# A long convolution ahead of two expert layers: merged loads, decodings in three parts, an earlier filter transform, and the first tile's last rows kept on chip

## The chip, the cores and the metric

One core of a Trainium2 chip runs the kernel. The metric is the time of one execution in microseconds (us) on the device. Engines are called as in the profile: PE (matmul), PEld (its weight loads), DVE (vector), ACT (scalar), POOL (GpSimd), SP (the queue that issues most DMAs). Each engine works through its own instruction list in order.

## What is computed

```python
h_filt = (np.maximum(pos_emb @ w1, 0) @ w2) * exp(-0.01 * pos)   # 12480 x 128
u = x * v
y = irfft(rfft(u, 2 * S) * rfft(h_filt, 2 * S))[:S]              # causal convolution
x = x * y
h = x @ w_in;  g = P(h) / (Q(h) + 1e-06);  x = g @ w_out         # 128 -> 2048 -> 128
h = x @ w_in2; g = where(h >= 1, h, where(h <= -1, 0, (h + 1) ** 2 / 4))
out = g @ w_out2
```

P is a cubic and Q a quadratic in h with the weights `a` and `b`. The four weight matrices of the two layers arrive as float64, two 32-bit words a number.

## The kernel before

The convolution is an FFT in factors 256 and 49, as matmuls. It is written as `conv_transform`, whose order is that of the code (no scheduler moves it), and the two layers are the main loop that follows.

**Load stage** (L126 to L234). 49 rows are taken in 14 chunks of 1, 2, 4 (eleven times) and 2 (`CHS`). For a chunk, `loads` (L141) issues three DMAs on SP: `pt` (positions), `xt` and `vt`. `products` (L151) multiplies x and v on POOL, `mlp` (L159) makes the filter's hidden layer on PE and DVE, `parts` (L170) splits the result `st` into a high part (ACT) and a low part (DVE), the first transform runs on PE, ACT and DVE copy it to `so`, and ACT issues the write of `so` to `sd` in DRAM. The buffers of x and v hold three chunks.

**Filter stage** (L237 to L376). `sd` is read back in 34 groups of frequencies (`groups`): one of 1, 31 of 4, two of 2. `load(g)` reads `ru` from `sd`, `load_g(g)` the tables `gg`; both are issued by SP. For a group: `R` (L251) transforms the filter's rows on PE and splits the result (ACT makes the high part, DVE the low one, L88), `AB` (L260) applies w2, `U` (L274) transforms the signal on PE into the PSUM tile `up` (one buffer), `M` (L285) multiplies both on DVE (L298 to L302) and combines on POOL (L300 to L305), `Tr` transposes, `Inv` (L323) transforms back, and `co` is written to `cd` in DRAM. The steps are a software pipeline: step s works on group s + 1 in AB, s in U and M, s + 2 in R, s - 2 in Tr, s - 3 in Inv.

**Decodings.** `decode_steps` (L44) turns one block of the float64 weights `b` into float32 with six operations on DVE (`t`, `a`, `t`, `t`, then `k` and the last product) and an addition on POOL in their middle; for w_in blocks ACT then makes a high part and POOL the low one (L410 to L416). There are 32 such blocks. `fill(i)` (L106) first does the part behind the addition of block i - 1, then the part ahead of it of block i. Two run ahead of the steps, two in each of steps -2 and -1, and one in each step from 0 on, so that they end in step 25.

**Hand-over and main loop.** The column sums of the last weight matrix (`colsum`, L430) are made in the three tail steps. Then `X0` (L482) reads a tile of x (`xTt`) and of `cd` (`ct`) from DRAM, `XF` makes the last transform on PE, `XM` (L501) multiplies by x on DVE, `XH` and `XL` split it. The main loop takes 196 items of 1024 columns in the order of `ORDER`; in each, `h1` is the first layer's product on PE and `n1` (L551) the first of five operations on DVE. The second layer follows 11 items later.

Of the kernel before, what the change touches and what calls it, by code (L numbers as in the profile page):

```python
# [16 lines left out]
D = 128  # L17
# [13 lines left out]
CSP = [(0,), (1,), (2, 3)]  # L31
# [12 lines left out]
def decode_steps(nc, pool, src, n, dst):  # L44
# [32 lines left out]
def conv_transform(tc, ident, io, cd, fillers, colsum):  # L77
# [3 lines left out]
    xp, vp, posT, w1, w2, win, sgn, f1c, ggc = io  # L81
    with ExitStack() as ctx:
# [43 lines left out]
        with tc.tile_pool(name="ca", bufs=2) as ca, tc.tile_pool(name="cap", bufs=1, space=PSUM) as cap:  # L126
            xr = xp.rearrange("(b p m) d -> p b m d", b=NB, p=N1)
            vr = vp.rearrange("(b p m) d -> p b m d", b=NB, p=N1)
# [12 lines left out]
            def loads(c):  # L141
                m0, n = first[c], CHS[c]
                b = buf[c] = {}
                b["p"] = ca.tile([128, mx, N1], F32, name="pt", tag="pt", bufs=4)
                b["x"] = ca.tile([N1, NB, mx, D], F32, name="xt", tag="xt", bufs=XB)
                b["v"] = ca.tile([N1, NB, mx, D], F32, name="vt", tag="vt", bufs=XB)
                nc.sync.dma_start(b["p"][:, 0:n], posT[:, m0:m0 + n, :])
                nc.sync.dma_start(b["x"][:, :, 0:n], xr[:, :, m0:m0 + n, :])
                nc.sync.dma_start(b["v"][:, :, 0:n], vr[:, :, m0:m0 + n, :])

            def products(c):  # L151
# [3 lines left out]
                for k in range(NB):  # L155
                    nc.gpsimd.tensor_tensor(st[:, 0:n, k * 256:k * 256 + D], b["x"][:, k, 0:n], b["v"][:, k, 0:n],
                                            op=ALU.mult)

            def mlp(c):  # L159
# [3 lines left out]
                for j in range(n):  # L163
                    nc.tensor.matmul(rv[:, j], b["p"][:, j], w1b, start=True, stop=True)
# [25 lines left out]
            loads(3)  # L190
# [131 lines left out]
        def Inv(g, h):  # L322
# [4 lines left out]
            if h == 0:  # L327
                e["co"] = grp.tile([SL, 4, 256], F32, name="co", tag="co")
# [19 lines left out]

        for s in range(-2, ng + 3):
# [8 lines left out]
            on(R, s + 2)  # L358
# [18 lines left out]
def kernel(ctx, tc, xp, vp, xT, posT, w1, w2, win, sgn, f1c, ggc, fic,  # L377
# [390 lines left out]
```

## Time and profile before

| what | us |
|---|---|
| median of 3 runs (1693.29 to 1694.32) | 1693.93 |
| the profiled execution | 1693.96 |
| its span, first to last instruction | 1692.2 |
| PE busy in the span | 1581.5 (93%) |
| DVE busy | 1506.0 (89%) |
| ACT busy | 1426.9 (84%) |
| POOL busy | 1439.9 (85%) |

The page's first table gives busy time per engine over the whole span, which mixes three short stages and a long loop. To see what a stage is limited by one reads the windows (busy time of each engine in a stretch, with PE's granted clock and the share of the DMA engines), then the timeline of one engine: start, duration, instruction, and in brackets how long the engine was idle just before and what ended it.

### The profile page before, as it was taken

How to read it: one execution, taken by the hardware profiler on the slowest of the kernel's cores; microseconds unless marked ns; L12 is line 12 of the kernel's file. 1: busy time of each engine (PE TensorE's matmuls, PEld its weight loads, DVE VectorE, ACT ScalarE, POOL GpSimd, SP SyncE). 2: the span in 40 equal slices, each digit the busy share in tenths (PEclk: the TensorE clock that was granted, in tenths of full speed). 3: DMA queues.
4: the chain of work that ended last, by engine and by line, in shares of the span. 5: the costliest groups of instructions: out<-in, count | busy, mean ns of one | idle time of the engine just before them, and what ended most of it. 6: DMA issues, size and time to landing. Idle time of an engine off the chain costs nothing.

```text
span 1692.2 us, 18487 instructions
## 1 busy us (share of the span) xinstructions
PE 1581.5 (93%) x6310; PEld 1063.8 (63%) x6310; DVE 1506.0 (89%) x1524; ACT 1426.9 (84%) x1665; POOL 1439.9 (85%) x883
## 2 busy tenths in 40 slices
PE   6758888986799999999999999999999999999999
PEld 5747777873456656666666666566666666666566
DVE  5549999828999999999999999999999999999990
ACT  4433454546799999999999999999999999999996
POOL 4315676636599999999999999999999999999996
PEclk9877999999899999999999999999999999999999
DMA  9975777631000000000000000000000000000000
GB/s 337 380 259 174 217 216 218 173 100 38 19 13 25 25 1 25 26 26 25 13 13 25 25 26 26 1 25 26 25 25 26 0 26 25 26 16 7 0 7 16
DMA packets 59996, 113.20 MB, mean 67 GB/s; under 512 B 4599, under 2 KB 36607, under 8 KB 58493
## 3 DMA queue, kind: packets, MB, share of 16 engines
q1 hardware_dynamic: 45064, 80.35, 15.4%
q10 hardware_dynamic: 14724, 31.53, 5.1%
q8 instruction: 50, 0.82, 0.2%
q14 instruction: 46, 0.37, 0.1%
q0 software_dynamic: 112, 0.13, 0.0%
HBM read 73.46 MB, written 38.54 MB: 66 GB/s over the span
## 4 chain that ended last, share of the span: by engine, by line
PE 73%; DVE 13%; ACT 6%; DMA 5%; issue 2%; POOL 1%; SPq 0%; ACTq 0%; DVEq 0%; POOLq 0%
PE acc L479 36%; PE h L473 10%; PE h L475 10%; PE h L474 9%; PE acc L496 3%; DMA sd<-so 2%; PE up L281 2%; DVE m L299 1%; DVE m L302 1%; DMA vt<-in_vp_dram 1%; PE cp L334 1%; ACT z L537 1%; DVE t L67 1%; ACT f L533 1%; DVE n L555 1%
## 5 line engine op out<-in xcount | busy, mean ns | idle before, releaser
L546 POOL TENSOR_TENSOR w<-w,z 128x1024 f32<-128x1024 f32 x196 | 470.5, 2400 | 12.3
L632 POOL TENSOR_TENSOR y<-y,c 128x1024 f32<-128x1024 f32 x196 | 468.9, 2393 | 9.8 <-ACT c L628 4.7
L479 PE MATMUL acc<-g,wo 128*128 128x512 f32 (+1 forms) x800 | 373.2, 590 | 12.5 <-DVE g L576 12.5
L479 PE MATMUL acc<-y,wo 128*128 128x512 f32 (+1 forms) x800 | 368.0, 584 | 1.0 <-DVE o L642 0.9
L542 POOL TENSOR_SCALAR w<-z,ab 128x1024 f32<-128x1024 f32 x196 | 235.1, 1199 | 39.9 <-ACT z L537 38.8
L479 PEld LDWEIGHTS acc<-y,wo 128*128 128x128 f32 x800 | 151.6, 190 | 181.4 <-issue 173.0
L576 DVE SCALAR_TENSOR_TENSOR g<-r,n 128x1024 f32<-128x1024 f32 x196 | 240.1, 1225 | 20.7 <-PE h L475 0.5
L555 DVE SCALAR_TENSOR_TENSOR n<-n,co,h 128x1024 f32<-128x1024 f32 x196 | 250.9, 1280 | 6.1
L567 DVE SCALAR_TENSOR_TENSOR n<-n,co,r 128x1024 f32<-128x1024 f32 x196 | 250.2, 1277 | 1.8 <-ACT r L563 1.3
L551 DVE SCALAR_TENSOR_TENSOR n<-f,co,h 128x1024 f32<-128x1024 f32 x196 | 249.5, 1273 | 0.2 <-ACT f L533 0.2
L571 DVE SCALAR_TENSOR_TENSOR r<-w,r 128x1024 f32<-128x1024 f32 x196 | 239.6, 1222 | 0.0
L563 ACT ACTIVATE r<-L 128x1024 f32<-128x1024 f32 x196 | 213.3, 1088 | 20.5 <-DVE g L576 20.5
L479 PEld LDWEIGHTS acc<-g,wo 128*128 128x128 f32 x800 | 149.8, 190 | 123.3 <-issue 93.9
L473 PE MATMUL h<-x1hi,hi 128*128 128x512 f32 (+1 forms) x400 | 214.0, 535 | 13.7 <-DVE n L555 6.8
L559 ACT ACTIVATE L<-w 128x1024 f32<-128x1024 f32 x196 | 216.8, 1106 | 0.0
L615 ACT ACTIVATE y<-h 128x1024 f32<-128x1024 f32 x196 | 210.7, 1075 | 4.6 <-PE h L475 4.5
L537 ACT ACTIVATE z<-h 128x1024 f32<-128x1024 f32 x196 | 208.1, 1062 | 6.0 <-PE h L475 4.6
L533 ACT ACTIVATE f<-h 128x1024 f32<-128x1024 f32 x196 | 208.3, 1063 | 0.0
L473 PE MATMUL h<-x2hi,hi 128*128 128x512 f32 (+1 forms) x400 | 159.3, 398 | 5.9 <-DVE n L555 5.8
L626 ACT ACTIVATE c<-c 128x1024 f32<-128x1024 f32 x147 | 164.7, 1120 | 0.0
L621 ACT ACTIVATE c<-y 128x1024 f32<-128x1024 f32 x147 | 163.8, 1114 | 0.6
L475 PE MATMUL h<-x1lo,hi 128*128 128x512 f32 (+1 forms) x400 | 155.6, 389 | 0.6 <-POOL x1lo L512 0.6
(93 smaller groups left out, 2615.6 us busy)
## 6 DMA issues: line engine op xcount, KB each, us to landing
ru<-sd SPq DMA_DIRECT2D x31, 588.0 KB
sd<-so ACTq DMA_DIRECT2D x11, 1536.0 KB
ct<-cd SPq DMA_DIRECT2D x24, 512.0 KB
cd<-co ACTq DMA_DIRECT2D x30, 392.0 KB
gg<-in_ggc_dram SPq DMA_DIRECT2D x31, 300.1 KB
xTt<-in_xT_dram SPq DMA_DIRECT2D x24, 256.0 KB
out_dram<-o SPq DMA_DIRECT2D x24, 256.0 KB
xt<-in_xp_dram SPq DMA_DIRECT2D x11, 512.0 KB
```

The costliest lines, as they stand in the source:

```text
L473: nc.tensor.matmul(o, hi[:, f], x[0], start=True, stop=False)
L475: nc.tensor.matmul(o, hi[:, f], x[1], start=False, stop=True)
L479: nc.tensor.matmul(ps, W[l][2][:, f], g[:, k * w:(k + 1) * w], start=f == 0, stop=f == NF - 1)
L533: nc.scalar.activation(s1[i]["f"], s1[i]["h"], AF.Copy, scale=ra3)
L542: nc.gpsimd.tensor_scalar(s["w"], s["z"], ab[:, 1:2], ab[:, 0:1], op0=ALU.mult, op1=ALU.add)
L546: nc.gpsimd.tensor_tensor(s["w"], s["w"], s["z"], op=ALU.mult)
L551: nc.vector.scalar_tensor_tensor(s["n"], s["f"], a[2], s["h"], op0=ALU.add, op1=ALU.mult)
L555: nc.vector.scalar_tensor_tensor(s["n"], s["n"], a[1], s["h"], op0=ALU.add, op1=ALU.mult)
L567: nc.vector.scalar_tensor_tensor(s["n"], s["n"], a[0], s["r"], op0=ALU.add, op1=ALU.mult)
L571: nc.vector.scalar_tensor_tensor(s["r"], s["w"], 1.000001, s["r"], op0=ALU.add, op1=ALU.mult)
L576: nc.vector.scalar_tensor_tensor(s["g"], s["r"], 2.0, s["n"], op0=ALU.subtract, op1=ALU.mult, reverse0=True)
L632: nc.gpsimd.tensor_tensor(s["y"], s["y"], s["c"], op=ALU.add)
```

## The change

Loads: x, v and the positions are interleaved in DRAM, and one DMA reads a chunk of all three. Decodings: each is in three parts (ahead of POOL's addition, behind it, and the split), each done in a later `fill`; seven buffers for `b`; three run ahead of the steps, 23 in steps 2 to 33, four behind the tail steps and two behind the first tile's product. Filter transform: `R(s + 2)` stands behind `AB` and ahead of `Tr`, `U` and `M`. First tile: the rows that the last three groups make for it are copied from `co` to `ct0` in SBUF; the others are read from `cd` earlier; `begin` takes the place of the first `XF`, `XM`, `XH`, `XL`. `colsum` goes to item 8 of the main loop.

```diff
-CSP = [(0,), (1,), (2, 3)]
+PRE = 3
+POST = 4, 2
...
-        e["b"] = pool.tile([128, n, 2], I32, name="b64", tag="b64", bufs=3)
+        e["b"] = pool.tile([128, n, 2], I32, name="b64", tag="b64", bufs=7)
...
-        def fill(i):
-            nonlocal late
-            for fn in late:
-                fn()
-            late = []
-            fill_load(i + 2)
-            if i < len(fills):
+        def fill(n=1):
+            nonlocal done
+            for i in range(done, done + n):
+                fill_load(i + 1)
+                later()
                 for fn in fills[i][1:6]:
                     fn()
-                late = fills[i][6:]
+                waiting.append([fills[i][6:8], fills[i][8:]])
+                fill_load(i + 4)
+            done += n
+
+        def later():
+            for parts in waiting:
+                for fn in parts.pop(0):
+                    fn()
+            waiting[:] = [parts for parts in waiting if parts and parts[0]]
...
-                nc.sync.dma_start(b["p"][:, 0:n], posT[:, m0:m0 + n, :])
-                nc.sync.dma_start(b["x"][:, :, 0:n], xr[:, :, m0:m0 + n, :])
-                nc.sync.dma_start(b["v"][:, :, 0:n], vr[:, :, m0:m0 + n, :])
+                b["a"] = ca.tile([128, mx, 5, 128], F32, name="xt", tag="xt", bufs=XB)
+                nc.sync.dma_start(b["a"][:, 0:n], xvp[:, m0:m0 + n])
...
-                if c + 4 < nch:
-                    loads(c + 4)
+                if 3 < c + 3 < nch:
+                    loads(c + 3)
...
-                if c == nch - 4:
-                    for g in range(5):
-                        load_g(g)
-                    fill_load(0)
-                    fill_load(1)
+                if c == nch - 3:
+                    load_g(0)
+                    load_g(1)
+                    fill_load(PRE + 2)
...
-                e["co"] = grp.tile([SL, 4, 256], F32, name="co", tag="co")
+                e["co"] = grp.tile([SL, 4, 256], F32, name="co", tag="co", bufs=3)
...
             if h + 2 == n:
+                if g >= ng - TQ:
+                    for i in range(n):
+                        nc.sync.dma_start(ct0[k0 + i:k0 + i + 1], e["co"][0:TILES[0], i])
                 (nc.scalar if g < ng - TQ else nc.sync).dma_start(cdr[:, k0:k0 + n], e["co"][:, 0:n])
+                if g == ng - TQ:
+                    nc.sync.dma_start(ct0[0:k0], cd[0:k0, 0:TILES[0] // NB])
...
         for g in range(5):
             load(g)
-        for i in range(2):
-            fill(i)
-        done = 2
+            if g > 1:
+                load_g(g)
+        fill(PRE)
...
+        mid = len(fills) - PRE - sum(POST)
         for s in range(-2, ng + 3):
             if 5 <= s + 5 < ng:
                 load(s + 5)
                 load_g(s + 5)
             on(AB, s + 1)
+            on(R, s + 2)
             if s < ng:
                 on(Tr, s - 2, 0)
             on(U, s)
             on(M, s)
-            on(R, s + 2)
...
-                if s == ng:
-                    cs = ps.tile([128, 2, 512], F32, name="cs", tag="ap")[:, 0, 0:1]
-                for part in CSP[s - ng]:
-                    colsum(cs, part, 4)
-            for i in range(2 if s < 0 else 1):
-                fill(done)
-                done += 1
+            elif 0 < s and s * mid // (ng - 1) > (s - 1) * mid // (ng - 1):
+                fill()
+            if s == ng - 1:
+                fill_load(len(fills))
+        fill(POST[0])
+        begin(ps.tile([128, 2, 512], F32, name="x0", tag="ap")[:, 0, 0:TILES[0] * 128], ct0, xt0)
+        fill(POST[1])
+        while waiting:
+            later()
...
+    def begin(p, ct0, xt0):
+        for j in range(TILES[0]):
+            for r in range(2):
+                nc.tensor.matmul(p[:, j * 128:(j + 1) * 128], ct0[:, j // NB, r, j % NB * D:(j % NB + 1) * D],
+                                 fit[:, r], start=r == 0, stop=r == 1)
+        nc.vector.tensor_tensor(xt0, p, xt0, op=ALU.mult)
+        nc.scalar.copy(x10[0], xt0)
+        nc.gpsimd.tensor_tensor(x10[1], xt0, x10[0].bitcast(F32), op=ALU.subtract)
...
-        X0(0)
+        x1[0] = x10
         X0(1)
-        XF(0)
-        XM(0)
-        XH(0)
-        XL(0)
         for i in range(n + 24):
+            if i == 8:
+                colsum()
```

The order of instructions at three places. On SP, between the last chunks' loads and the `ru` loads; `b` are blocks of weights. Before:

```order
L147 DMA pt<-in_posT_dram 128x256
L148 DMA xt<-in_xp_dram 128x2x256
L149 DMA vt<-in_vp_dram 128x2x256
L121 DMA gg<-in_ggc_dram 98x196
L121 DMA gg<-in_ggc_dram 98x784 x4
L56 DMA b_782<-in_w_in_dram 128x512
L56 DMA b_784<-in_w_out_dram 128x2x256
L248 DMA ru<-sd 98x384
L248 DMA ru<-sd 98x4x384 x4
```

and with the change:

```order
L158 DMA xt<-in_xvp_dram 128x2560 x11
L158 DMA xt<-in_xvp_dram 128x1280
L136 DMA gg<-in_ggc_dram 98x196
L136 DMA gg<-in_ggc_dram 98x784
L57 DMA b_777<-in_w_in_dram 128x512
L57 DMA b_779<-in_w_out_dram 128x2x256
L57 DMA b_781<-in_w_in_dram 128x512
L57 DMA b_783<-in_w_out_dram 128x2x256
L57 DMA b_785<-in_w_in_dram 128x512
L256 DMA ru<-sd 98x384
L256 DMA ru<-sd 98x4x384 x2
L136 DMA gg<-in_ggc_dram 98x784
```

Three issues a chunk became one, three `gg` loads moved behind the `ru` loads, and three `b` loads moved ahead of them.

On DVE, one step of the filter stage (M is the four operations on `up`, `rs` the split of R). Before:

```order
L298 TENSOR_TENSOR m_2827<-up,ab 128x392
L299 TENSOR_TENSOR m_2825<-up,ab 128x784
L301 TENSOR_TENSOR m_2828<-up,ab 128x392
L302 TENSOR_TENSOR m_2826<-up,ab 128x784
L88 TENSOR_TENSOR rs_2844<-rp_2838,rs_2843 128x392
L72 TENSOR_SCALAR k<-b_2626 128x256
L73 SCALAR_TENSOR_TENSOR w_2865<-k,t 128x256
L67 TENSOR_SCALAR t<-b_2708 128x256
L68 TENSOR_SCALAR a<-b_2708 128x256
L69 SCALAR_TENSOR_TENSOR t<-b_2708,t 128x256
L70 SCALAR_TENSOR_TENSOR t<-b_2708,t 128x256
```

and with the change:

```order
L89 TENSOR_TENSOR rs_2617<-rp_2611,rs_2616 128x392
L306 TENSOR_TENSOR m_2638<-up,ab 128x392
L307 TENSOR_TENSOR m_2636<-up,ab 128x784
L309 TENSOR_TENSOR m_2639<-up,ab 128x392
L310 TENSOR_TENSOR m_2637<-up,ab 128x784
L73 TENSOR_SCALAR k<-b_2288 128x256
L74 SCALAR_TENSOR_TENSOR wo_78<-k,t 128x256
L68 TENSOR_SCALAR t<-b_2368 128x256
L69 TENSOR_SCALAR a<-b_2368 128x256
L70 SCALAR_TENSOR_TENSOR t<-b_2368,t 128x256
L71 SCALAR_TENSOR_TENSOR t<-b_2368,t 128x256
```

The split stands ahead of M, so the decoding follows M directly; in ten of the steps from 1 to 33 the decoding is missing.

On DVE, the hand-over: the last M and the first operations behind it (XM is L501 before, L460 with the change). Before:

```order
L298 TENSOR_TENSOR m_3488<-up,ab 128x196
L299 TENSOR_TENSOR m_3486<-up,ab 128x392
L301 TENSOR_TENSOR m_3489<-up,ab 128x196
L302 TENSOR_TENSOR m_3487<-up,ab 128x392
L501 TENSOR_TENSOR xTt<-acc_3595,xTt 128x512 x2
L551 SCALAR_TENSOR_TENSOR n<-f,co,h_3619 128x1024
```

and with the change, from the last of the four decodings to the middle of the next:

```order
L73 TENSOR_SCALAR k<-b_3382 128x256
L74 SCALAR_TENSOR_TENSOR w_3472<-k,t 128x256
L68 TENSOR_SCALAR t<-b_3384 128x256
L69 TENSOR_SCALAR a<-b_3384 128x256
L70 SCALAR_TENSOR_TENSOR t<-b_3384,t 128x256
L71 SCALAR_TENSOR_TENSOR t<-b_3384,t 128x256
L460 TENSOR_TENSOR xt_95<-x_3481,xt_95 128x512
L73 TENSOR_SCALAR k<-b_3384 128x256
L74 SCALAR_TENSOR_TENSOR wo_78<-k,t 128x256
L68 TENSOR_SCALAR t<-b_3386 128x256
L69 TENSOR_SCALAR a<-b_3386 128x256
L70 SCALAR_TENSOR_TENSOR t<-b_3386,t 128x256
```

Where nothing stood between the last M and XM, the last step's decoding and four more do now, and two more stand between XM and the first L579 (n1).

## Rows read from the trace of the kernel before

**Rows 1.** DMA queues from 20 to 50 us (packets, MB, share of 16 engines).

```profile
q1 hardware_dynamic: 3636, 6.93, 61.5%
q10 hardware_dynamic: 544, 5.31, 42.0%
```

**Rows 2.** Windows of the three early stages: busy us (instructions), granted clock, DMA share, GB/s.

```profile
0.00:16.00 16.00, 7.29 (x33) 6.29 (x34) 5.00 (x14) 4.20 (x7) 5.60 (x14) 1.00 0.77 225
112.00:142.00 30.00, 18.36 (x70) 17.15 (x71) 16.74 (x44) 4.05 (x9) 8.96 (x14) 0.50 0.68 199
145.00:150.00 5.00, 3.44 (x25) 2.90 (x25) 4.68 (x8) 0.85 (x2) 3.07 (x4) 1.00 0.44 122
160.00:200.00 40.00, 36.16 (x247) 31.55 (x246) 39.31 (x62) 20.07 (x36) 27.25 (x30) 1.00 0.75 212
...
400.00:440.00 40.00, 28.01 (x82) 14.61 (x82) 39.20 (x34) 25.21 (x27) 25.07 (x15) 0.91 0.06 20
```

**Rows 3.** Timeline of ACT near the end of the load stage.

```profile
79.12 0.58 ACT L221 COPY so<-sp 128x512 f32<-128x512 f32 x1 [8.43 <-DMA vt<-in_vp_dram]
```

**Rows 4.** Timelines of SP and PE in the change-over.

```profile
109.91 2.56 SPq L248 DMA_DIRECT2D ru<-sd  x5
...
112.42 0.72 PE L256 MATMUL rp<-gg,ru 98*128 98x98 f32 x2 [8.45 <-DMA ru<-sd]
...
114.79 1.99 PE L256 MATMUL rp<-gg,ru 98*128 98x98 f32 x8
125.70 0.70 PE L267 MATMUL ap<-rs,w2h 128*128 128x392 f32 x1 [8.92 <-ACT rs L87]
...
127.83 1.01 PE L281 MATMUL up<-gg,ru 98*128 98x98 f32 x4
...
134.11 3.57 PE L281 MATMUL up<-gg,ru 98*128 98x98 f32 x16
```

**Rows 5.** Timeline of DVE in the change-over.

```profile
121.99 0.29 DVE L67 TENSOR_SCALAR t<-b 128x256 int32<-128x256 int32 x1 [7.54 <-DMA b<-in_w_in_dram]
...
124.52 0.29 DVE L67 TENSOR_SCALAR t<-b 128x256 int32<-128x256 int32 x1
...
137.79 0.57 DVE L298 TENSOR_TENSOR m<-up,ab 128x392 f32<-128x392 f32 x1 [2.27 <-PE up L281]
```

**Rows 6.** Timeline of DVE, one step of the filter stage, M to M.

```profile
298.88 0.56 DVE L298 TENSOR_TENSOR m<-up,ab 128x392 f32<-128x392 f32 x1
...
301.58 0.56 DVE L88 TENSOR_TENSOR rs<-rp,rs 128x392 fp32r<-128x392 f32 x1
302.06 0.79 DVE L72 TENSOR_SCALAR k<-b 128x256 int32<-128x256 int32 x1
...
306.44 0.56 DVE L298 TENSOR_TENSOR m<-up,ab 128x392 f32<-128x392 f32 x1
```

**Rows 7.** Timeline of POOL in the same step: the last product operation.

```profile
303.63 1.21 POOL L305 TENSOR_TENSOR z<-m,m 128x392 f32<-128x392 f32 x1
```

**Rows 8.** Timeline of DVE: two steps without a decoding.

```profile
333.62 0.57 DVE L298 TENSOR_TENSOR m<-up,ab 128x392 f32<-128x392 f32 x1 [3.06 <-PE up L281]
...
339.95 0.57 DVE L298 TENSOR_TENSOR m<-up,ab 128x392 f32<-128x392 f32 x1 [3.06 <-PE up L281]
```

**Rows 9.** Timeline of DVE from the last M to the main loop.

```profile
360.70 0.36 DVE L298 TENSOR_TENSOR m<-up,ab 128x196 f32<-128x196 f32 x1 [1.94 <-POOL z L305]
...
380.89 0.69 DVE L501 TENSOR_TENSOR xTt<-acc,xTt 128x512 f32<-128x512 f32 x1 [18.61 <-PE acc L496]
...
388.86 1.27 DVE L551 SCALAR_TENSOR_TENSOR n<-f,co,h 128x1024 f32<-128x1024 f32 x1
```

**Rows 10.** Timeline of PE: the first tile's last transform.

```profile
377.21 3.48 PE L496 MATMUL acc<-fit,ct 128*128 128x128 f32 x16 [5.93 <-DMA xTt<-in_xT_dram]
```

**Rows 11.** Chain of waits at the hand-over: the last write (start, duration).

```profile
370.29 2.26 DMA cd<-co
```

More of the change, by code (lines that the diff above doesn't have):

```diff
@@ L74, in decode_steps, with conv_transform @@
     ]
-def conv_transform(tc, ident, io, cd, fillers, colsum):
+def conv_transform(tc, ident, io, cd, fillers, xT, begin):
     nc = tc.nc
-    xp, vp, posT, w1, w2, win, sgn, f1c, ggc = io
+    xvp, w1, w2, win, sgn, f1c, ggc = io
     with ExitStack() as ctx:
@@ L94, in conv_transform @@
         w2l = big.tile([128, NB, D], F32R, name="w2l")
+        ct0 = big.tile([NK, TILES[0] // NB, 2, NB * D], F32, name="ct0")
+        xt0 = big.tile([128, TILES[0] * 128], F32, name="xt0")
+        nc.gpsimd.dma_start(xt0, xT[:, 0:TILES[0] * 128])
         ggp = pool("cv_gg", 1)
@@ L99, in conv_transform, with fill_load @@
         fills = fillers(pool("cv_fill", 1))
-        late = []
-        def fill_load(i):
-            if i < len(fills):
-                fills[i][0]()
-        def fill(i):
-            nonlocal late
-            for fn in late:
-                fn()
-            late = []
-            fill_load(i + 2)
-            if i < len(fills):
+        waiting = []
+        loaded = done = 0
+        def fill_load(k):
+            nonlocal loaded
+            for fn in fills[loaded:k]:
+                fn[0]()
+            loaded = max(loaded, min(k, len(fills)))
+        def fill(n=1):
[3 more added lines that the diff above has]
+                later()
                 for fn in fills[i][1:6]:
                     fn()
-                late = fills[i][6:]
+                waiting.append([fills[i][6:8], fills[i][8:]])
[6 more added lines that the diff above has]
+            waiting[:] = [parts for parts in waiting if parts and parts[0]]
         def load_g(g):
@@ L155, in products @@
                 for k in range(NB):
-                    nc.gpsimd.tensor_tensor(st[:, 0:n, k * 256:k * 256 + D], b["x"][:, k, 0:n], b["v"][:, k, 0:n],
+                    nc.gpsimd.tensor_tensor(st[:, 0:n, k * 256:k * 256 + D], b["a"][:, 0:n, k], b["a"][:, 0:n, NB + k],
                                             op=ALU.mult)
@@ L163, in mlp @@
                 for j in range(n):
-                    nc.tensor.matmul(rv[:, j], b["p"][:, j], w1b, start=True, stop=True)
+                    nc.tensor.matmul(rv[:, j], b["a"][:, j, 4], w1b, start=True, stop=True)
                 for k in range(NB):
@@ L189, in conv_transform @@
             loads(2)
-            loads(3)
             nc.scalar.dma_start(w2b[0:64, 0], w2)
@@ L195, in conv_transform @@
             mlp(0)
+            loads(3)
             parts(0, 0)
@@ L366, in conv_transform, with kernel @@
                 on(Tr, s - 2, 2)
-                if s == ng:
-                    cs = ps.tile([128, 2, 512], F32, name="cs", tag="ap")[:, 0, 0:1]
-                for part in CSP[s - ng]:
-                    colsum(cs, part, 4)
-            for i in range(2 if s < 0 else 1):
-                fill(done)
-                done += 1
+            elif 0 < s and s * mid // (ng - 1) > (s - 1) * mid // (ng - 1):
[7 more added lines that the diff above has]
+            later()
 @with_exitstack
-def kernel(ctx, tc, xp, vp, xT, posT, w1, w2, win, sgn, f1c, ggc, fic,
+def kernel(ctx, tc, xvp, xT, w1, w2, win, sgn, f1c, ggc, fic,
                           w_in1, w_out1, ca, cb, w_in2, w_out2, out):
@@ L427, in fillers, with colsum @@
         return parts
-    def colsum(pt, part, parts):
-        for f in range(part * NF // parts, (part + 1) * NF // parts):
+    def colsum():
+        pt = banks[1][:, 0:1]
+        for f in range(NF):
             nc.tensor.matmul(pt, W[1][2][:, f], ones, start=f == 0, stop=f == NF - 1)
-        if part == parts - 1:
-            nc.scalar.activation(bias, pt, AF.Copy, scale=-1.0)
+        nc.scalar.activation(bias, pt, AF.Copy, scale=-1.0)
+    x10 = [cp.tile([128, TILES[0] * 128], F32R, name=f"x10{k}") for k in range(2)]
+    def begin(p, ct0, xt0):
[6 more added lines that the diff above has]
+        nc.gpsimd.tensor_tensor(x10[1], xt0, x10[0].bitcast(F32), op=ALU.subtract)
     with tc.manual_schedule():
-        conv_transform(tc, ident, (xp, vp, posT, w1, w2, win, sgn, f1c, ggc), cd, fillers, colsum)
+        conv_transform(tc, ident, (xvp, w1, w2, win, sgn, f1c, ggc), cd, fillers, xT, begin)
     nc.scalar.activation(ab, co[:, 4:6], AF.Abs)
```

11 lines of the change are left out of this document (3 added, 8 removed).

## The prediction, before the change was run

> **What bounds the kernel now.** The main loop is out of reach of the change: it begins with the first tile's product and runs 1300 of the span's 1692 us at one pace. What counts is when it starts. I read the windows of 40 us first, then the DMA queues, the chain of waits and each engine's timeline in the three stages ahead of it.
>
> The load stage (to 110 us) keeps the DMA engines full: in the stretch from 20 to 50 us the loads' queue and the writes' queue together fill 103% of sixteen engines, loads at 6.93 MB in 18.45 us of all engines (376 GB/s), writes of `sd` at 5.31 MB in 12.6 us (421 GB/s); the sum is 408 GB/s [rows 1]. In the first 16 us it is only 225 [rows 2]. Near the end ACT waits 8.43 us, and the trace names the last load of `vt` as what ended it [rows 3].
>
> The change-over (110 to 138 us) waits. The first `ru` load is issued at 109.91, the first full-size M starts at 137.79; between them PE waits 8.92 us for ACT's half of R(1)'s split, which stands on ACT behind the cast of a decoded weight, and that decoding waits 7.54 us on DVE for its own load [rows 4, 5]. PE has the 1.2 GHz level throughout (granted clock 0.50) [rows 2].
>
> The filter stage (138 to 361 us) is DVE's: 39.31 of 40 us busy from 160 to 200 [rows 2]. A step there is M (2.70 us), the split of a later R (0.48) and one decoding (4.38 in the step shown) [rows 6]. Alone, a decoding takes 2.53 [rows 5]; in the step it is drawn out, and POOL's last product operation runs until 304.84, 5.96 us after M's start [rows 6, 7]. After step 25 no decodings are left and steps take 6.33 us, DVE waiting 3.06 of them for PE's U [rows 8]: that is PE's own pace.
>
> The hand-over: from M(33) at 360.70 to the first tile's product XM(0) at 380.89, and to the first main-loop operation of DVE at 388.86 [rows 9]. The last 6.9 us before PE's first product at 377.21 are the last `cd` write (2.26 us) and the reload [rows 10, 11]. From 400 to 440 us DVE is again full (39.20 of 40), so a later start is not made up there [rows 2].
>
> **The change part by part**, against the profiled execution (1693.96 us; the runs shown have a median of 1693.93, so nothing is to be shifted).
>
> *Loads, three in one.* The same bytes, in 10 KB runs per partition where they were 2 KB, with one issue for three. All loads are 49 x 128 x 2560 B = 16.06 MB: at 376 GB/s 42.7 us, at the writes' 421 GB/s 38.1, so 4.6 less if the longer runs go like the writes, which have 12 KB runs. The first three chunks, now in 512 B and 1 KB runs, come to 3.6 MB in 16 us; at 408 GB/s this would be 8.8 us plus some 2.5 to the first byte, 4.7 less; I take 4, as the first products still wait for their chunk. Fewer chunks in flight (3 for 4 of `pt`) costs nothing while the queue stays full. SP issues `gg` 2 and `b` 5 times ahead of the `ru` loads, for 5 and 2; about the same bytes. ACT's 8.43 us wait stays, since the write still follows the last load. Sum -8.5. Bounds: -3, if only the start gains, and -14.5, if the wait mostly goes too.
>
> *Change-over.* Two and a half decodings, their data already there, run while the last `sd` write lands; none stands between R and M in steps -2 to 1. The work left from the `ru` issue T to M(1) is PE's, at 1.2 GHz: R(0) starts at T+2.5, R(1) ends by 6.9, its split takes 0.5, AB(1) 2.1, R(2) 1.9, U(0) 1.0, AB(2) 2.1, R(3) 1.9 (now ahead of U), U(1) 3.5 [rows 4]: T+19.9. Up to R(3) 2.6 MB must land, 13 us at the 199 GB/s of this stretch [rows 2]; R(3) has its turn at 14.5, so the loads come just in time. Before it was 27.9, so -8.0. Bounds: 0, if another load is waited for, and -12.
>
> *Filter stage to XM(0).* 23 decodings now fall on steps 2 to 33, mostly two steps in three, and the split goes ahead of M. A step with a decoding: POOL's products still run to 5.96 us after M's start and hold up the first operations; the three behind them take about 1.2, so it ends near 7.15; with the next split 7.63 from M to M. A step without: 2.70 + 0.48 = 3.18. So DVE falls 1.3 behind PE's 6.33 in one step, 2.6 in two, and catches up in the third. PE feels it only where U finds `up` not yet read: U, at the upper level half of its 3.57 [rows 4], starts 1.8 before the next M's turn, 4.5 after this one; M ends at 2.70, so a lag of some 1.85 is free. Per three steps PE loses about 0.75: 6.58 on average. M(1) to M(31): 30 x 6.58 = 197.4. The last three steps all have decodings: 2.70 + 4.3, then 1.5 (M at half size) + 4.3 = 12.8 to M(33). Then M(33) 1.5, its decoding 3.0, four more of 2.6 = 10.4, ahead of XM(0). With 1.0 for the first steps at the lower clock the sum is 226.1; before it was 380.89 - 137.79 = 243.1. So -17.0. Bounds: -24.5, if no lag reaches PE (30 x 6.33), and -9.0 (first rival).
>
> *First tile on chip.* A write and a reload of 6.9 us become one small transfer of about 2.7 (the 2.26 of the last write and one more issue): 4.2 less on that path. But XM(0) then waits for DVE's four decodings, 14.9 us after M(33), while the transfer path comes to 13 to 16; so this is inside the sum above and gives nothing more. Its cover gone (no decodings there), it would give the 4.2.
>
> *The rest.* The two last decodings, 5.1 us, lie between XM(0) and DVE's first loop operation, 8.0 us apart, while PE makes h1: nothing. The column sums leave the tail (within the path just priced) and go to item 8, where PE is busy 28.01 of 40 us: nothing, at most 4 if DVE waits for that h1. The third part of a decoding only delays POOL's subtraction by one.
>
> Sum: -8.5 - 8.0 - 17.0 = -33.5, so 1660.5; I say **1660**.
>
> **Two rules of the Trainium skill against this.** First, the rows: a decoding takes 4.38 us beside POOL's operations and 2.53 alone [rows 5, 6]. The page "SBUF — State Buffer", section "Who interferes with whom", says that DVE and GpSimd hold one port pair as an exclusive lock for a whole instruction, the other being fully blocked. By it a decoding's end hangs on POOL's end and gains nothing from an earlier start: the first rival, 1668 for 1660. Second, the row: 408 GB/s in the load stage [rows 1]. The page "DMA: Bandwidth & Descriptors", section "Specifications", gives about 358 GB/s as the HBM limit of a core. The trace is already above it, so it can't be this kernel's ceiling; that the stage has reached some other one is the second rival, 1666 for 1660.
>
> **The rivals.**
> 1. *POOL pins the decodings.* A decoding ends at 7.56 after M, as now, and the next split comes on top: 8.04. The lag after two is 3.42, PE loses 1.55 per three steps, 6.85 on average: 30 x 0.27 = +8.1, 1668. For it speaks how the operations stretch up to POOL's ends; against it that `k` now starts before POOL's third operation. 0.20.
> 2. *The load stage is at its ceiling.* Engines already 103% busy; longer runs don't help, only the start gains: +5.5, 1666. Against it speaks the writes' 421 beside the loads' 376. 0.12.
> 3. *All lag is hidden, and the ACT wait goes.* -7.5 and -6: 1647. For it: DVE's total has room, two decodings in three steps leave 0.6 of 19 us. 0.15.
> 4. *Slower: PE stays at 1.2 GHz in the filter stage.* With DVE no longer the pace, PE's level sets the step: it would be about 12.2 instead of 6.33, +5.9 per step. From six such steps on the 33.5 are eaten; at twelve it is 1731. For it: PE works the whole change-over at 0.50 [rows 2]. Against: from 145 to 150 us it has 1.00, and keeps it through a stage in which it works 36 of 40 us, less than it then will [rows 2]. 0.03.
> 5. *It doesn't do what it says:* what is gained ahead is waited for at the loop's start, within 3 us of before. 0.02.
>
> **How the numbers follow.** My forecast, 1660, has 0.48. Its neighbours 1, 2 and 3 (1668, 1666, 1647) hold 0.47. The range 1645 to 1674 takes these in, with the first two partly together; outside lie case 4, case 5 and what is left of the bounds all at one end. A measurement of this kernel can tell about 0.2% (3.4 us) from no change. Faster 0.95, same 0.02, slower 0.03: only cases 4 and 5 are not faster.
>
> **What would show it.** Right: the first `ru` issue near 101 us; M(1) some 20 us after it; in the filter stage PE above 38 of 40 us busy, steps with a decoding about 7.6 and the pair's third short; XM(0) about 226 us behind M(1), with DVE busy up to it and not waiting for the transfer; main loop at the old pace. Wrong: a load stage ending after 106 (case 2), a mean step of 6.8 or more (case 1), 6.4 or less (case 3), a granted clock of 0.5 beyond 10 us into the filter stage (case 4), XM(0) waiting for `ct0`, or a gap at item 8.

## The result and the profile after

The changed kernel takes **1670.12 us** (median of 4 runs, 1669.52 to 1671.09), the kernel before 1694.12 beside it: ratio 0.9855, 95% interval 0.9838 to 0.9872. That is 24 us less, where 33.5 were forecast; 1670 lies in the range, 10 above the forecast. The profiled span is 1667.6 us for 1692.2. The stages are read from the one profiled execution of each kernel.

| stage (us) | before | after | change | forecast |
|---|---|---|---|---|
| start to first `ru` issue | 109.91 | 105.61 | -4.3 | -8.5 |
| to M(1) | 27.88 | 16.28 | -11.6 | -8.0 |
| M(1) to M(33) | 222.91 | 213.75 | -9.2 | }-17.0 |
| M(33) to XM(0) | 20.19 | 15.89 | -4.3 | } |
| XM(0) to n1 | 7.97 | 11.17 | +3.2 | 0 |
| n1 to the end | 1303.3 | 1304.9 | +1.6 | 0 |

The timelines of SP and of DVE, changed kernel: the rows that answer to [rows 4, 5, 9]. L306 is M's first operation, L460 XM(0), L579 n1.

```profile
105.61 1.27 SPq L256 DMA_DIRECT2D ru<-sd  x3
```

and DVE's:

```profile
121.89 0.57 DVE L306 TENSOR_TENSOR m<-up,ab 128x392 f32<-128x392 f32 x1 [0.77 <-PE up L289]
...
335.64 0.35 DVE L306 TENSOR_TENSOR m<-up,ab 128x196 f32<-128x196 f32 x1
...
351.19 0.42 DVE L71 SCALAR_TENSOR_TENSOR t<-b,t 128x256 int32<-128x256 int32 x1
351.53 0.68 DVE L460 TENSOR_TENSOR xt<-x,xt 128x512 f32<-128x512 f32 x1
...
359.48 0.69 DVE L529 TENSOR_TENSOR xTt<-acc,xTt 128x512 f32<-128x512 f32 x1 [0.78 <-PE acc L524]
360.09 0.41 DVE L74 SCALAR_TENSOR_TENSOR wo<-k,t 128x256 f32<-128x256 int32 x1
362.70 1.28 DVE L579 SCALAR_TENSOR_TENSOR n<-f,co,h 128x1024 f32<-128x1024 f32 x1 [2.20 <-ACT f L561]
```

DVE has its decodings up to XM(0) and does not wait for the transfer, as forecast; what it waits for on the way is POOL's addition, 0.63 to 0.70 us in three decodings and 1.67 in one. Behind XM(0) something new stands: n1 waits for ACT's f, f for ACT's z, and z, as ACT's timeline shows, for the last operation of the last decoding (L74), which stands on DVE behind the *second* tile's product (L529):

```profile
360.67 1.02 ACT L565 ACTIVATE z<-h 128x1024 f32<-128x1024 f32 x1 [2.92 <-DVE wo L74]
```

The windows that answer to [rows 2] and the two queues that answer to [rows 1], from 20 to 50 us:

```profile
0.00:16.00 16.00, 5.73 (x22) 4.51 (x22) 3.56 (x11) 3.62 (x6) 7.47 (x16) 1.00 0.77 283
20.00:50.00 30.00, 25.22 (x138) 22.78 (x138) 19.14 (x36) 14.96 (x26) 10.08 (x8) 0.94 1.01 408
112.00:142.00 30.00, 26.18 (x162) 23.72 (x162) 20.79 (x35) 9.46 (x17) 14.85 (x19) 0.84 0.95 239
160.00:200.00 40.00, 38.45 (x279) 35.43 (x277) 36.15 (x55) 21.90 (x40) 27.59 (x31) 1.00 0.78 224
```

and the queues:

```profile
q1 hardware_dynamic: 732, 6.68, 56.1%
q10 hardware_dynamic: 593, 5.55, 44.4%
```

The loads' own queue went from 376 to 397 GB/s (6.68 MB in 56.1% of 30 us), the writes from 421 to 417, and the sum stayed at 408. In the filter stage PE is now busy 38.45 of 40 us and DVE has 3.85 to spare: the pace passed to PE, but not wholly, as the waits of PE from 122 to 336 us say (releaser, us in total, times, longest):

```profile
PE up L289 <- DVE m L310: 10.9, 14, 1.4
PE ap L278 <- DVE rs L89: 1.5, 2, 1.3
```

### The profile page after: what moved, and what is told of

Read it like the earlier page. It is cut to its first block, busy times and chain, and to the rows that moved or that the text cites. A ratio compares the mean times of both kernels' runs of the same rounds, so it can differ in the third digit from the quotient of the medians.

```text
span 1667.6 us, 18467 instructions
## 1 busy us (share of the span) xinstructions
PE 1577.8 (95%) x6310; PEld 1062.9 (64%) x6310; DVE 1505.3 (90%) x1524; ACT 1429.0 (86%) x1665; POOL 1437.6 (86%) x884
## 4 chain that ended last, share of the span: by engine, by line
PE 68%; ACT 5%; DVE 4%; issue 2%; DVEq 0%; ACTq 0%
PE acc L507 36%; PE h L501 10%; PE h L502 10%; PE h L503 10%; PE acc L524 2%; ACT f L561 1%; DVE n L579 1%; DVE n L583 1%; ACT z L565 1%; ACT c L649 1%; ACT y L643 1%; DVE n L595 1%; DVE r L599 1%; ACT c L654 1%; ACT L L587 1%
## 5 line engine op out<-in xcount | busy, mean ns | idle before, releaser
L579 DVE SCALAR_TENSOR_TENSOR n<-f,co,h 128x1024 f32<-128x1024 f32 x196 | 249.6, 1274 | 2.2 <-ACT f L561 2.2
L501 PE MATMUL h<-x1hi,hi 128*128 128x512 f32 (+1 forms) x384 | 206.9, 539 | 6.1 <-ACT y L643 5.4
L501 PE MATMUL h<-x2hi,hi 128*128 128x512 f32 (+1 forms) x400 | 159.2, 398 | 5.8 <-DVE n L583 5.8
L503 PE MATMUL h<-x2lo,hi 128*128 128x512 f32 (+1 forms) x400 | 154.6, 386 | 0.0
```

The source lines that it names most:

```text
L501: nc.tensor.matmul(o, hi[:, f], x[0], start=True, stop=False)
L503: nc.tensor.matmul(o, hi[:, f], x[1], start=False, stop=True)
L579: nc.vector.scalar_tensor_tensor(s["n"], s["f"], a[2], s["h"], op0=ALU.add, op1=ALU.mult)
```

## The experiments

Each kernel is the changed one with the edit shown. Ratios are to the kernel before on the same chip (0.9855 for the changed kernel; 0.001 is 1.7 us). Stages are read as in the table. Nine of the profiles have the load stage as changed: their first `ru` issue lies between 104.5 and 106.9 us, so what lies inside this band is no finding.

**Three loads a chunk** (e1).

```diff
-                nc.sync.dma_start(b["a"][:, 0:n], xvp[:, m0:m0 + n])
+                nc.sync.dma_start(b["p"][:, 0:n], posT[:, m0:m0 + n, :])
+                nc.sync.dma_start(b["x"][:, :, 0:n], xr[:, :, m0:m0 + n, :])
+                nc.sync.dma_start(b["v"][:, :, 0:n], vr[:, :, m0:m0 + n, :])
...
```

> The changed kernel with the loads of a chunk as three DMAs again (2 KB runs), everything else as changed. Theory A, the load stage is set by the bytes that full DMA engines move, and the merged loads only fill them sooner: the stretch from 20 to 50 us shows 400 to 410 GB/s again, the first 16 us fall from 283 to about 225 GB/s, the first ru load is issued at 109 to 111 us (105.61 with merged loads), and the stages behind it keep their lengths, so the time is 1670.1 + 4 = about 1674. Theory B, my forecast's, the long runs make the loads' queue faster: 376 GB/s or less for the loads' own queue in that stretch, for 397, and the first ru load at 112 or later. Theory C, the merged loads give nothing and the earlier ru load comes from the other order of gg and b loads at the stage's end: first ru load below 107.

Ratio 0.9875 (0.9858 to 0.9891). The stretch has 409 GB/s, its loads 376; the first 16 us 244. The first `ru` issue is at 108.02, 2.4 later than in the changed kernel and 1.1 beyond the band: between A and C. So the longer runs do make the loads' queue faster, and the stage gets no more bytes a second from it.

**Fewer bytes** (e2). The host puts the positions first, and chunks 4 to 7 load three fifths of a row; `x` stands in for the missing `v` there, so the output is another one.

```diff
+                q = 3 if c in LESS else 5
-                nc.sync.dma_start(b["a"][:, 0:n], xvp[:, m0:m0 + n])
+                nc.sync.dma_start(b["a"][:, 0:n, 0:q], xvp[:, m0:m0 + n, 0:q])
...
```

> Four chunks (4 to 7) load three fifths of their bytes (v is left out and x is used for it, so the convolution's input is another one there): 4 x 0.52 = 2.1 MB less. Theory A, full DMA engines set the load stage: 2.1 MB at 408 GB/s are 5.1 us, so the first ru load is issued at 100 to 102 us for 105.61 and the time falls by about 5, to 1665. Theory B, the waits of ACT for so's two buffers (the latency of a write, not its bytes) set it: less than 1.5 us, 104 to 106 and 1669 to 1670.

First `ru` issue at 103.13, some 2.4 earlier: half of what A asks, more than B allows. But the edit also cut the runs of these chunks to 1.5 KB. Its window from 20 to 50 us and the loads' queue there:

```profile
20.00:50.00 30.00, 25.13 (x135) 23.90 (x136) 19.58 (x37) 14.36 (x24) 9.52 (x9) 0.90 0.99 374
q1 hardware_dynamic: 1775, 5.72, 54.6%
```

The engines are as full as before (0.99) and move 374 GB/s for 408; the loads go at 349 GB/s (5.72 MB in 54.6% of 30 us) for 397. So less engine time was taken away than the bytes say, and the run does not tell A from B. And the ratio is 0.9854, none of it left: M(1) came at 121.34, since the change-over took 18.2 us for 16.3.

**No decoding in the steps** (e5): `PRE = 26`, with the `b` loads ahead of the stage left at five.

> 26 decodings ahead of the steps for 3, so none stands in steps 2 to 33. The change-over grows by 23 decodings of 3 to 3.5 us, 70 to 80 us, and the time with it; what counts is M(1) to M(33), 213.7 us now. Theory A, what these steps take beyond PE's own 6.33 us a step is the decodings' lag reaching PE: 199 to 203 us, M to M 6.3 to 6.4 throughout. Theory B, the filter transform ahead of M or PE's own work sets the pace and decodings are hidden: 210 or more.

One run, 1723.63 us, as the change-over took 88 us. M(1) to M(33) 193.5 us, with 6.31 from M to M nearly throughout from M(5) on: A, and lower than it said. So of the 213.7 us some 18 are what decodings cost there (20.2, less 2.3 for a lapse of PE's clock in the changed kernel's profile, shown in the next section).

**The third part ahead of M** (e6). `rest` does the third part of a decoding whose second part is done.

```diff
         for s in range(-2, ng + 3):
+            rest()
```

> The third part of a decoding (ACT's cast and POOL's subtraction lo) is issued at the head of the next step, ahead of M, and not behind M's four POOL operations. Steps with a decoding take 7.24 us without lo and 7.77 with it now, and three steps 20.0 for 19.0 at PE's own pace. Theory A, the lo subtraction, which stands on POOL behind M's operations and holds up DVE's next decoding by 0.53, is what makes the lag long enough to reach PE: all steps with a decoding take 7.25, three steps 19.3 to 19.6, M(1) to M(33) 208 to 211 us for 213.7, time 1665 to 1667. Theory B, the lag reaches PE anyhow: 213 to 214 us, 1669 to 1670.

Ratio 0.9824 (0.9808 to 0.9841); M(1) to M(33) **207.6**, 6.1 less: A, and a little lower than it said. Of the 6.1, 2.3 are PE's clock, which fell in the changed kernel's profile there and not in this one (its windows stand in the next section), so 3.9 are the edit's. First the timeline of POOL of the changed kernel, from M's last two operations on, and DVE's of the same step:

```profile
160.35 0.95 POOL L312 TENSOR_TENSOR z<-m,m 128x392 f32<-128x392 f32 x1
161.27 1.08 POOL L313 TENSOR_TENSOR z<-m,m 128x392 f32<-128x392 f32 x1
162.31 0.78 POOL L430 TENSOR_TENSOR lo<-w,hi 128x256 fp32r<-128x256 f32 x1
```

```profile
161.38 1.13 DVE L69 TENSOR_SCALAR a<-b 128x256 int32<-128x256 int32 x1
162.42 0.95 DVE L70 SCALAR_TENSOR_TENSOR t<-b,t 128x256 int32<-128x256 int32 x1
163.41 0.42 DVE L71 SCALAR_TENSOR_TENSOR t<-b,t 128x256 int32<-128x256 int32 x1
```

and the two of this experiment, same step:

```profile
155.23 0.73 POOL L438 TENSOR_TENSOR lo<-w,hi 128x256 fp32r<-128x256 f32 x1
156.37 0.95 POOL L315 TENSOR_TENSOR m<-m,m 128x392 f32<-128x392 f32 x1 [0.42 <-DVE m L314]
...
159.67 1.08 POOL L320 TENSOR_TENSOR z<-m,m 128x392 f32<-128x392 f32 x1
```

```profile
159.78 1.12 DVE L69 TENSOR_SCALAR a<-b 128x256 int32<-128x256 int32 x1
160.82 0.41 DVE L70 SCALAR_TENSOR_TENSOR t<-b,t 128x256 int32<-128x256 int32 x1
```

In the first pair DVE's operations end with POOL's: `a` at 162.51 with the second `z` (162.35), L70 at 163.37 only behind `lo` (163.09). In the second, `lo` runs before M's products need POOL, and L70 takes 0.41 for 0.95. Steps with a decoding take 7.24 for 7.24 and 7.77 in turn, and PE's waits for M fall from 10.9 us to 3.7.

**R behind M** (e3): `on(R, s + 2)` moved back behind `on(M, s)`.

> The changed kernel with R(s + 2) behind M again, decodings placed as changed. Theory A, R ahead of M takes DVE's lag off the path: with R behind, AB at the head of PE's next step waits for the split that stands behind M on DVE, as in the kernel before (18.9 us of such waits), so each step with a decoding costs its full 7.24 to 7.77 and the others PE's 6.31: M(1) to M(33) 222 to 231 us for 213.7, time 1678 to 1688. Theory B, the spread of the decodings alone does it and the place of R nothing: 212 to 216 us, within 3 us of 1670. In the change-over R(3) no longer stands ahead of U(1): first ru issue to M(1) 1 to 2 us shorter than 16.3, if PE's clock rises as early.

Ratio 0.9912 (0.9890 to 0.9934); M(1) to M(33) 224.3 us: A. Waits of PE, from 122 to 346 us:

```profile
PE ap L278 <- DVE rs L89: 14.7, 20, 1.5
```

A step without a decoding takes 6.25 for 4.98: with the split behind M it catches up nothing. Two of its steps are longer than others at the same place in the pattern (8.64 for 7.05, 7.91 for 6.25), where PE's granted clock was 0.50 (131 to 141 and 329 to 339 us): some 3 of the 10.6 us by which this stretch is longer. The change-over stayed at 16.16, where 1 to 2 less was expected.

**Decodings at their old places** (e4).

```diff
...
-            elif 0 < s and s * mid // (ng - 1) > (s - 1) * mid // (ng - 1):
-                fill()
+            if done < len(fills):
+                fill(2 if s < 0 else 1)
+            else:
+                later()
```

> The changed kernel with the decodings where they stood before: two ahead of the steps, two in each of steps -2 and -1, one in each step until they are out, none behind the tail. Theory A, the places make the gain: first ru issue to M(1) 25 to 29 us for 16.3 (PE waits for the split of R(1) behind a decoding again), M(1) to M(33) 222 to 230 for 213.7 (lag in 25 steps without a break), XM(0) to the first loop operation of DVE 7.5 to 8.5 for 11.2, in sum 1683 to 1693. Theory B, R ahead of M is what counts: change-over below 20 us and M(1) to M(33) below 218, time below 1676.

Ratio 0.9949 (0.9934 to 0.9965). Change-over 26.3 us, M(1) to M(33) 224.0, XM(0) to n1 8.1: A in all three. Rows of PE and DVE in its change-over show the waits of before again, somewhat shorter (8.92 and 7.54 us there):

```profile
124.44 1.02 PE L278 MATMUL ap<-rs,w2h 128*128 128x392 f32 x2 [5.80 <-DVE rs L89]
```

```profile
120.10 0.29 DVE L68 TENSOR_SCALAR t<-b 128x256 int32<-128x256 int32 x1 [5.08 <-DMA b<-in_w_in_dram]
```

M(1) to M(33) took 222.9 us before, 224.3 with the new places alone, 224.0 with R ahead alone, and 213.7 with both; some 3 of the 224.3 and 2.3 of the 213.7 are PE's clock. Neither half of this pair gains more than about 2 us there by itself.

**First tile through DRAM** (e7).

```diff
-                if g >= ng - TQ:
-                    for i in range(n):
-                        nc.sync.dma_start(ct0[k0 + i:k0 + i + 1], e["co"][0:TILES[0], i])
...
-                if g == ng - TQ:
-                    nc.sync.dma_start(ct0[0:k0], cd[0:k0, 0:TILES[0] // NB])
+                if g == ng - 1:
+                    nc.sync.dma_start(ct0, cd[:, 0:TILES[0] // NB])
```

> The changed kernel with the first tile's rows all read back from DRAM behind the last cd write (one reload, nothing copied from co on chip). Theory A, the transfer path and DVE's four decodings end together now, so the longer path shows: XM(0) 3 to 5 us later, M(33) to XM(0) 19 to 21 us for 15.9, time 1673 to 1675. Theory B, my forecast's, DVE's decodings decide XM(0) and the copy on chip is worth nothing: M(33) to XM(0) 16 to 17.5, time within 1.5 us of 1670.

M(33) to XM(0) 18.37, 2.5 more: between the two. PE's transform of the tile ended 18.3 us behind M(33) for 15.3, and DVE was idle 1.13 us for it; the other 1.4 are DVE's decodings, one of which waited 2.94 us for POOL's addition for 1.67. Ratio 0.9863 (0.9842 to 0.9885), not to be told from the changed kernel's.

**All six ahead of the product** (e9): `POST = 6, 0`.

> All six last decodings ahead of the first tile's product, none behind it. Theory A, ACT's first z waits for the last decoding (its memory is that of the closed pools), and that is what draws out the stretch from XM(0) to DVE's first loop operation: 7.8 to 8.6 us for 11.2, while M(33) to XM(0) grows from 15.9 to 21 to 22.5; in sum the loop starts 2 to 4 us later, 1672 to 1674. Theory B, the stretch is PE's (1.2 GHz, two tiles' last transforms) and the decodings are hidden in it: it stays at 10.5 to 11.5, and the time rises by the whole 5 to 6, to 1675 or more.

XM(0) to n1 8.37, M(33) to XM(0) 22.26: A. ACT's z waits for PE now:

```profile
360.68 1.02 ACT L565 ACTIVATE z<-h 128x1024 f32<-128x1024 f32 x1 [3.34 <-PE h L503]
```

From M(33) to n1 that is 30.6 us for 27.1: the last decodings are DVE's work on either side of XM(0). The time did not rise to A's 1672 to 1674: the ratio is 0.9855 all the same. In the profiled execution 2.3 of the 3.6 us came back in the filter stage, where the step that PE's clock drew out to 7.25 in the changed kernel took 4.98.

**Interleaved last decodings** (f1), together with e6's edit, `POST = 5, 1`.

```diff
-                later()
+                if not first:
+                    later()
                 for fn in fills[i][1:6]:
                     fn()
+                if first:
+                    later()
```

> The third part of a decoding ahead of M, as in the run before (1664.8, XM(0) at 347.26 and the first loop operation of DVE at 358.08 there), and the six last decodings interleaved: the part ahead of POOL's addition of one stands ahead of the two last operations of the one before, so DVE no longer waits 0.63 to 0.71 us in each; five of them ahead of the first tile's product, one behind it. Theory A, z waits for the last decoding and DVE's waits on POOL in the tail cost what the rows show: XM(0) at 347 to 348, as the transfer path ends it, XM(0) to the first loop operation 7.9 to 8.8 us for 10.8, so 1661.5 to 1663. Theory B, the product of the second tile and PE's level hold the start of the loop: stretch 10 or more, 1664 to 1666.

Ratio 0.9828 (0.9814 to 0.9841), not to be told from e6's; the time is 1664.28, B's. XM(0) to n1 is 7.95, so z's wait is gone, as A says; but XM(0) came at 351.18, 18.0 us behind M(33), not at 347 to 348. DVE's waits on POOL turned into longer operations, as its timeline and POOL's show:

```profile
344.69 0.28 DVE L73 TENSOR_SCALAR k<-b 128x256 int32<-128x256 int32 x1
345.08 0.84 DVE L74 SCALAR_TENSOR_TENSOR wo<-k,t 128x256 f32<-128x256 int32 x1
```

```profile
344.91 0.72 POOL L72 TENSOR_TENSOR t<-t,a 128x256 int32<-128x256 int32 x1 [1.75 <-DVE t L71]
```

L74 takes 0.41 to 0.43 alone, and here ends 0.29 behind POOL's addition of the *next* decoding. M(33) to n1 is 26.0 for 27.1: 1.1 gained, and lost in a change-over of 20.1 us (below).

**Later b loads** (f2) and **column sums at item 4** (f3), both on top of f1: the loads are issued by ACT behind the tenth `sd` write; `if i == 4` for `if i == 8`.

> As the kernel before it in this list, with the five b loads of the load stage (1.31 MB) issued by ACT behind the sd write of the tenth chunk (about 81 us), where the DMA engines soon run out of work, and not by SP at 68 to 75 us, where they are full. Theory A, the bytes ahead of a write in the full engines set when so comes free: the sd write of the ninth chunk lands 3 us sooner, ACT's wait of 3.97 us at 83.64 goes, and the first ru load is issued at 102 to 103.5 for 105 to 107; M(1) comes 1 to 3 us sooner. Theory B, that wait is the write's own latency: 104.5 or later, no change in the time.

> As the first kernel of this list, with the column sums at item 4 of the main loop for item 8, where their 3.4 us stand on PE right ahead of the third tile's last transform. Theory A, at item 8 they push PE back where the second layer begins (the loop falls 0.75 us behind the kernel before at items 12 to 14): the time from the first to the last loop operation of DVE falls by 0.5 to 1 us. Theory B, they are hidden at either place: within 0.3 us.

f2: first `ru` issue at 107.29, 2.8 later than f1's; ratio 0.9835. Its ninth and tenth `sd` writes came 1.8 and 1.2 us sooner than in f1, the later ones 1.6 to 2.7 later. These are B's numbers, but no test of B: issuing the five loads took ACT itself 4.3 us between 80.13 and 84.52, so that one wait made room for another, as ACT's timeline in f2 shows ("issue" is time in which it waited for nothing that the profile shows).

```profile
84.62 0.58 ACT L240 COPY so<-sp 128x512 f32<-128x512 f32 x1 [5.78 <-issue]
```

f3: n1 to the end 1304.6 us, 1304.5 at item 8; ratio 0.9833. B.

**PE kept at work** (f4), on top of e6 and the interleaving, `POST = 4, 2`.

```diff
+        wm = ps.tile([128, 2, 512], F32, name="wm", tag="up")
+        for _ in range(40):
+            nc.tensor.matmul(wm[:, 0, 0:128], ident, ident, start=True, stop=True)
         for g in range(5):
             load(g)
```

> Two things beside the third part ahead of M, told apart by their stages. First, 40 matmuls without use (identity times identity into a PSUM tile that nobody reads) stand on PE between the load stage and R(0), where PE was idle for 8.5 us and its granted clock fell from 1.00 to 0.50. The stretch from the first ru issue to M(1) took 16.2 to 20.1 us in the runs so far, 16.2 where the clock was back at 1.00 8 us behind R(0) and 20 where it stayed at 0.50. Theory A, PE's work at the lower level sets the stretch: with the clock at 1.00 throughout it is 11 to 14 us. Theory B, the landing of ru and gg sets it, and the clock only adds where it stays low: 15 to 16.5 us. Theory C, the clock falls all the same: 16 to 20. Second, the interleaved tail with four decodings ahead of the first tile's product and two behind it (five and one gave 25.96 us from M(33) to DVE's first loop operation, four and two without interleaving 27.4): 24 to 25.5 if XM(0) comes 15.5 to 16.5 us behind M(33) with the transfer path, 26 or more if the two behind it still hold z. In sum 1657 to 1661 by A, 1660 to 1663 by B.

**1662.18 us, ratio 0.9813** (0.9800 to 0.9827), the lowest of all: better than the kernel before, and by about 7 us (0.9813 to 0.9855) than the changed one. Most of this is e6's edit, 0.9824 by itself; what the matmuls add does not show in the ratios, only in the stage. Windows of PE (busy, granted clock, DMA share, GB/s) in the changed kernel:

```profile
114.00:116.00 2.00, 2.00 (x9) 0.50 0.94 255
116.00:118.00 2.00, 1.87 (x13) 0.86 0.93 257
118.00:120.00 2.00, 2.00 (x16) 1.00 0.93 242
```

in f1:

```profile
114.00:116.00 2.00, 2.00 (x10) 0.50 0.93 270
116.00:118.00 2.00, 2.00 (x10) 0.50 0.95 281
118.00:120.00 2.00, 2.00 (x9) 0.50 0.92 290
```

and in f4, where it never left 1.00:

```profile
114.00:116.00 2.00, 2.00 (x17) 1.00 0.94 300
116.00:118.00 2.00, 1.87 (x14) 1.00 0.93 290
118.00:120.00 2.00, 2.00 (x21) 1.00 0.92 298
```

And PE's timeline in f4:

```profile
101.31 9.17 PE L364 MATMUL wm<-ident 128*128 128x128 f32 x80 [1.28 <-DVE so L241]
110.32 0.36 PE L274 MATMUL rp<-gg,ru 98*128 98x98 f32 x2
```

The clock stays at 1.00. The stretch is 14.5 us, 0.5 over A's end and 0.5 under B's, but the matmuls were too many: R(0) began 4.58 behind the `ru` issue, where it began 2.78 behind it in the changed kernel (108.39 us). From R(0) to M(1) it took 9.96 us, for 13.50 there and 17.24 in e1. The tail gained nothing (27.4 us from M(33) to n1): with two decodings behind XM(0), z waits, here 1.03 us for POOL's `lo`.

## Why the prediction was right in its direction and 10 us off in size

**Loads: mis-sized, -8.5 for -4.3.** The step that failed is "4.6 less if the longer runs go like the writes". The loads' queue did get faster (376 to 397, and 376 again in e1), half way to the writes' 421, but all queues together moved 408 GB/s as before, so the full stretch gained nothing. That is the second rival. The 4 for the start was too much as well: its 3.6 MB are what all queues moved in the first 16 us (225 GB/s), while the first three chunks are 7 of 49 rows, 2.3 MB. That window rose from 225 to 283 GB/s, 0.93 MB more, or 2.3 us at 408 GB/s (an estimate). Merging is worth 2.4 of the 4.3 by e1, or 1.1 to 3.5 against the band of the nine profiles; the rest is within what repeated runs differ by, or the order of `gg` and `b`, not tried alone. What sets the end of this stage is not settled: e2 slowed the queue while it took bytes away, and f2 put a new wait in the place of the old.

**Change-over: right mechanism, then a clock that came back early.** -8.0 rested on PE at 1.2 GHz throughout and gave 19.9 us; e1 and f1, where the granted clock stayed at 0.50 through the stretch, took 19.8 and 20.1. The changed kernel's profile took 16.3, because the clock was back at 1.00 some 8 us behind R(0); the last section orders the profiles by this. e4 puts the wait for R(1)'s split back and with it 10 us: the freed decodings are what the term is made of.

**Filter stage to XM(0): -13.5 for -17.0.** Right: a pace set by PE with DVE's lag on top, in patterns of three steps, and about 7.5 for a step with a decoding (7.63 forecast). The step that failed is "the third part of a decoding only delays POOL's subtraction by one". It leaves the subtraction on POOL behind M's products, and there it holds up DVE's L70 by 0.54 in every second decoding; three steps take 20.0 (7.25, 7.77 and 4.98) for the 19.75 of the forecast. That is the first rival's mechanism, by another POOL operation than it named: the mean step from M(1) to M(31) is 6.74, for 6.58 forecast and the rival's 6.85. The page "SBUF — State Buffer" of the Trainium skill, section "Who interferes with whom", says that DVE and GpSimd share a port pair under an exclusive lock, and that a DVE instruction with two inputs in SBUF contends with a GpSimd instruction that reads SBUF. L70 and L74 have two such inputs (`b` and `t`, `k` and `t`), and the rows above agree: L70 takes 0.95 beside `lo` and 0.41 without, L74 0.84 beside POOL's addition and 0.41 to 0.43 alone.

Of the 3.5 us that were missed, 2.3 are PE's clock in one step. M(4) to M(5) took 7.25, where e9, with the same decodings in these steps, took 4.98; PE's granted clock had fallen to 0.50 ahead of it, as its windows in the changed kernel show:

```profile
136.00:138.00 2.00, 1.22 (x7) 0.76 0.94 224
138.00:140.00 2.00, 2.00 (x11) 0.50 0.94 229
140.00:142.00 2.00, 2.00 (x10) 0.50 0.95 226
142.00:144.00 2.00, 2.00 (x7) 0.53 0.91 217
```

From M(1) to M(33) e9 took 211.5 us, for 211.2 in the forecast (1.0, 197.4 and 12.8), and e6, with the subtraction moved, 207.6. So the place of the subtraction is worth 3.9. That 211.2 is met without the clock's part is luck: the threes came out longer, the last two steps shorter (11.7 for 12.8). The other 1.0 lies between M(33) and XM(0), 15.9 for 14.9, and is the third part again: `lo` waits on POOL for ACT's cast, which stands behind ACT's last copies of `co`, and the addition that DVE needs stands behind `lo`. The timelines of POOL and DVE in the changed kernel:

```profile
342.99 0.72 POOL L430 TENSOR_TENSOR lo<-w,hi 128x256 fp32r<-128x256 f32 x1 [2.09 <-ACT hi L427]
344.43 0.42 DVE L74 SCALAR_TENSOR_TENSOR w<-k,t 128x256 f32<-128x256 int32 x1 [1.67 <-POOL t L72]
```

**First tile on chip: "nothing more" was 1.1 us**, what DVE waited for PE in e7. DVE's decodings and the transfers end together: XM(0) starts at 351.53, and PE's transform of that tile ended at 350.89, as its timeline in the changed kernel shows.

```profile
347.14 3.75 PE L458 MATMUL x<-fit,ct 128*128 128x128 f32 x16 [5.15 <-DMA cd<-co]
```

**The rest: 0 was +3.2.** The step that failed is "the two last decodings lie between XM(0) and DVE's first loop operation: nothing". Their time fits, though they took 6.6 us up to XM(1) for the 5.1 forecast; but the loop's first ACT operation waits for the last of them, and that one stands behind POOL's addition and XM(1). That it waits because it takes over the closed stage's memory is my reading of the program; no run tests it apart. With none or one decoding there the stretch is 7.6 to 8.4 us (e9, e4, f1 to f3); with two, 10.5 to 11.6 in all others. The column sums cost nothing that shows, as forecast (f3); n1 to the end took 1303.0 to 1305.0 us in all runs, before 1303.3, so of +1.6 nothing can be put down to the change.

The misses (+4.2, +3.5, +3.2, +1.6) come to 12.5, less 3.6 for the clock: 8.9, the difference between 33.5 and 24.6. So the clock gave 3.6 in the change-over and took 2.3 in the filter stage, neither of them forecast. The first two rivals came true in part together; the fourth (PE at 1.2 GHz in the filter stage) only for some 6 us.

## What to carry to other kernels

Moving work off a waiting engine pays only when it has somewhere to catch up: spread decodings and an earlier split gave 9 us together and at most about 2 singly. When costing work on DVE, list what POOL does beside it, in order: here one subtraction, of much the same length at either place (0.78 and 0.73 us), cost 3.9 us in all at the one and not at the other. Where one stage hands over to the next, look for what waits for the old stage's last straggler: here the loop's first ACT operation did, so nothing "hidden" should have been last.

## What the runs showed that was not expected

The same instructions met different clocks. The changed kernel, e6, f3 and f1 have the same instructions of PE in the change-over, and PE was idle 8.4 to 8.5 us ahead of it in each. From the first `ru` issue to M(1) they took 16.3, 16.2, 18.4 and 20.1 us; the granted clock was back at 1.00 by 118 us in the first and at 0.50 until 128 in the last. Over all profiles in which PE went without that long wait for a decoding, the stretch follows the clock: back 8 to 9 us behind R(0) it took 16.2 to 16.8 (changed, e3, e6, e9, f2), 11 behind 17.4 (e7), 13 behind 18.2 and 18.4 (e2, f3), 21 behind 19.8 and 20.1 (e1, f1). What decides when it comes back isn't settled here. That it costs up to 4 us of a 1670 us kernel from run to run is shown, and that 40 idle-time matmuls ahead of the stretch keep it at 1.00 in the one profile taken.

The clock also fell within the filter stage, at other times in each run: to 0.50 from about 137 to 143 us in the changed kernel, from 207 to 214 in f2, in e6 and f4 not at all between M(1) and M(33). Where PE sets the pace, a step got longer by it (7.25 for 4.98 in the changed kernel, 8.67 for 5.56 in f2). In e4 it fell from 139 to 144 us and cost nothing: DVE set the pace there, and the steps stayed at 7.2 and 7.8. So a filter stage that differs by 2 or 3 us between two profiles says nothing of the edit until the clock has been looked at.
